# Attention and feed-forward gradients in one kernel: twelve weight-gradient stores go to another queue, three staging buffers in place of four

## The chip, the cores and the metric

The kernel runs on one core of a Trainium2 chip. The metric is device time in microseconds, the median over runs of one launch; a profile shows one execution in detail.

## The reference, cut

The forward pass is `x + A(xn) + B(xn)` with `xn = layernorm(x)`, `x` of 4 x 1 x 512. `A` is one decoding step of attention over the last 1024 of 4096 cached keys and values; `B` is a GELU-gated feed-forward layer of width 1792. Asked for are the output and its gradient by all weights and by both caches.

```python
W = min(4096, max(256, Sk // 4))                 # 1024 of 4096
q = (x @ wq).reshape(B, Sq, Hq, Dh)              # 4 batches, 32 heads of 128
k = jnp.repeat(k_cache[:, :, Sk - W:, :], rep, axis=1)   # 8 kv heads
v = jnp.repeat(v_cache[:, :, Sk - W:, :], rep, axis=1)
p = _softmax(einsum("bhqd,bhkd->bhqk", q, k) * Dh ** -0.5)
a = einsum("bhqk,bhkd->bhqd", p, v).reshape(B, Sq, Hq * Dh) @ wo
b = (_gelu(xn @ w_gate) * (xn @ w_up)) @ w_down
out, vjp = jax.vjp(lambda ...: x + a + b, A_x, A_k_cache, A_v_cache, A_wq, A_wo, B_w_gate, B_w_up, B_w_down)
return (out, *vjp(grad_out))
```

All data are bfloat16. The cache gradients have the full shape 4 x 8 x 4096 x 128: the last 1024 positions of each of the 32 (batch, head) regions hold values, the first 3072 are zero and must be written as zero.

## The kernel before

**What moves.** 30.68 MB are read and 81.01 MB written. Of the written bytes 50.33 MB are the zeros of out_2 and out_3 (`zeros`, from the constant tile `ztile`, in regions of 786 KB, up to four to a transfer), 16.8 MB the computed parts of these two outputs, the rest the weight gradients out_4 to out_8.

**Stages.** First the loads and the feed-forward part: `xnm` and `dym` (`xn` and `dy`, masked by row, L251 to L256, made on POOL), the hidden layer, `f_rows` (L691), which lays the hidden gradients out as rows (`a_r`, `dhg_r`, `dhu_r`), and pieces for out_8, out_6 and out_7 (`piece_d`, `piece_g`). Then a loop over NT = 4 groups of GP = 2 kv heads. Group t runs `masks`, `scores(t, 0)` (keys: PE transposes, then the scores), `softmax`, `scores(t, 1)` (values, for dP), `softmax_d` (its two hooks make dS and its transpose), `pre(t + 1)` for the next group's queries, `odq`, `fin`, then `load_next(t)`, which issues the loads of group t + 2 on POOL's queue.

**Background pieces.** A deque `bg` holds small pieces of work in order: one matmul, one copy out of PSUM by `evac` (ScalarE or VectorE, whichever has the smaller planned load), and after the last piece of a tile the store. `tick(n)` takes n of them and stands between the foreground steps. `dvdk(t, 0)` and `dvdk(t, 1)` (L529) append the pieces of dV and dK, two tiles each, here called dv0, dv1, dk0, dk1; a tile `stg` is 1 MB, takes eight pieces, and comes from the pool `stage` (L760). `dw(t)` (L551) appends the pieces of out_5 (two tiles `osb_o`) and out_4 (two tiles `osb_q`) of 512 KB each, four pieces to a tile, from the pool `outp` with four buffers (L82). They run during group t + 1, and for the last group at the end.

**Queues.** Zeros are issued by ScalarE (ACT) in its own order, at the places that `ZN` (L391) and the calls of `zeros(n)` give: after the second K step of a head in `scores`. SyncE (SP) issues the stores of stg, of the feed-forward outputs and of the small outputs; GpSimd (POOL) the loads from group 1 on and, up to group 2, the stores of `dw`. Each engine issues in program order and waits at a transfer whose data or tile is not ready. A tile that is written again first waits for the landing of the store that read it.

**Tiles that share memory.** `xnm`, `a_r`, `dhg_r` and `dhu_r` use tags of the attention part (`od_x`, `dST`, `E_f`, `Gt`, `dS_x`), so a later attention tile has to wait for their last reader. After the feed-forward part its pools are closed, and `stage` (four tiles of 8 KB per partition) and `wodd` (weights and caches of odd groups) take their memory.

Of the kernel before, what the change touches and what calls it, by code (L numbers as in the profile page):

```python
# [13 lines left out]
BF16 = mybir.dt.bfloat16  # L14
P = 128
# [3 lines left out]
def kernel(  # L19
# [27 lines left out]
    nc = tc.nc  # L47

    B, Sq, D = A_x.shape
# [3 lines left out]
    rep = Hq // G  # L53
# [3 lines left out]
    ND = D // P  # L57
# [4 lines left out]
    NT = G // GP  # L62
    HG = GP * rep
# [5 lines left out]
    CW = HG * Dh  # L69
# [7 lines left out]
    const = ctx.enter_context(tc.tile_pool(name="const", bufs=1))  # L77
    kvp = ctx.enter_context(tc.tile_pool(name="kvp", bufs=3))
    wres = ctx.enter_context(tc.tile_pool(name="wres", bufs=1))
    attw = ctx.enter_context(tc.tile_pool(name="attw", bufs=2))  # L80
# [10 lines left out]
    def evac(out, in_, n, half=False, eng=None):  # L91

        eng = "dve" if half else eng or ("act" if chain else None)
        ca, cd = (190 + n) / 1.2, (120 + (n / 2 if half else n)) / 0.96
        if eng is None:
            eng = "act" if load["act"] + ca <= load["dve"] + cd else "dve"
        load[eng] += ca if eng == "act" else cd
        if eng == "act":
            last.append(nc.scalar.copy(out=out, in_=in_))  # L99
            return last[-1]  # L100
        return nc.vector.tensor_copy(out=out, in_=in_)  # L101

    def store(eng, out, in_, kind, apart):

        d = eng.dma_start(out=out, in_=in_)
        for k in apart:
            tc.declare_no_dep(d.ins, group=k, reason="stores write disjoint parts of the outputs")
        tc.add_to_no_dep_group(kind, d.ins)
        return d
# [14 lines left out]
    wg_sb = ffn_w.tile([P, ND, F], BF16, name="wg_sb")  # L124
    nc.sync.dma_start(out=wg_sb[:], in_=B_w_gate.rearrange("(p c) f -> p c f", p=P))
    wu_sb = ffn_w.tile([P, ND, F], BF16, name="wu_sb")
# [8 lines left out]
    dy_b = const.tile([P, D], BF16, name="dy_b")  # L135
# [10 lines left out]
    msk_i = const.tile([P, rep], FP32, name="msk_i")  # L146
# [86 lines left out]
    xn_b = const.tile([P, D], BF16, name="xn_b")  # L233
# [13 lines left out]
                                  in_=tps[:].rearrange("p c (b r) -> p c b r", b=B)[:, :, :, 0:8])  # L247

    xnm2 = [attw.tile([P, rep // 2, D], BF16, name="xnm", tag=tag, bufs=1) for tag in ("od_x", "dST")]  # L251
    dym = ffn.tile([P, rep, D], BF16, name="dym")
    for src, dst in ((dy_b, [dym[:, i, :] for i in range(rep)]), (xn_b, [xnm2[i // 2][:, i % 2, :] for i in range(rep)])):
        for i in range(rep):
            nc.gpsimd.tensor_scalar(out=dst[i], in0=src[:], scalar1=msk_i[:, i:i + 1], scalar2=None,
                                    op0=ALU.mult)  # L256


# [64 lines left out]
    def tick(n):  # L323
        for _ in range(min(n, len(bg))):
            bg.popleft()()
# [225 lines left out]
    def dw(t):  # L551

        X = st[t]["X"]
        eng = nc.gpsimd if t + 1 < NT else nc.sync

        def piece_o(g, i, held):
            if i == 0:
                held["osb"] = outp.tile([P, rep, D], BF16, name="osb_o", tag="o")
            mps = ps_w.tile([P, D], FP32, name="dwo_ps", tag="w")
            nc.tensor.matmul(mps[:], lhsT=X[:].rearrange("p h d -> p (h d)")[:, g * rep + i:CW:HG], rhs=dyz[:], start=True, stop=True)  # L560
            evac(held["osb"][:, i, :], mps[:], 512)
            if i == rep - 1:
                store(eng, out=out_5[t * CW:(t + 1) * CW, :].rearrange("(p k) n -> p k n", k=HG)[
                    :, g * rep:(g + 1) * rep, :], in_=held["osb"][:], kind="rest", apart=["zeros", "rest"])

        def piece_q(c2, k, held):
            if k == 0:
                held["osb"] = outp.tile([P, 2, GP, rep * Dh], BF16, name="osb_q", tag="o")
            ci, g = k // GP, k % GP
            c = c2 * 2 + ci  # L570
            mps = ps_w.tile([P, rep * Dh], FP32, name="dwq_ps", tag="w")
            nc.tensor.matmul(mps[:], lhsT=xnz[:, c:D:ND],  # L572
                             rhs=X[:, g * rep:(g + 1) * rep, :].rearrange("p i d -> p (i d)"), start=True, stop=True)
            evac(held["osb"][:, ci, g, :], mps[:], 512)
            if k == 2 * GP - 1:
                store(eng,
                      out=out_4.rearrange("(p c) j -> p c j", c=ND)[:, c2 * 2:(c2 + 1) * 2, t * CW:(t + 1) * CW],
                      in_=held["osb"][:].rearrange("p c g j -> p c (g j)"), kind="rest", apart=["zeros", "rest"])

        for g in range(GP):  # L580
            held = {}
            for i in range(rep):
                bg.append(lambda g=g, i=i, held=held: piece_o(g, i, held))
        for c2 in range(ND // 2):
            held = {}
            for k in range(2 * GP):
                bg.append(lambda c2=c2, k=k, held=held: piece_q(c2, k, held))
# [26 lines left out]
    NF4 = (NF + 3) // 4  # L614
# [9 lines left out]
    def ftb(name):  # L624
        t_ = ffn.tile([P, 4 * NF4, B], BF16, name=name)
        nc.vector.memset(t_[:], 0.0)
        return t_
# [52 lines left out]
    aT_b = ftb("aT_b")  # L680
    nc.vector.tensor_tensor(out=aT_b[:, 0:NF, :], in0=gl[:], in1=hu, op=ALU.mult)
    dhuT_b = ftb("dhuT_b")
# [3 lines left out]
    dhgT_b = ftb("dhgT_b")  # L686
# [1 line left out]

    acc_sum(0, [(lambda c, fc=fc: wd_sb[:, fc, c * P:(c + 1) * P], aT_b[:, fc, :]) for fc in range(NF)])

    def f_rows(srcT, nm, tag):  # L691

        ps = od_ps[:]
        for f4 in range(NF4):
            for b in range(B):
                nc.tensor.matmul(ps[b * RB:b * RB + 4, f4, :], lhsT=srcT[:, 4 * f4:4 * f4 + 4, b], rhs=ident[:],
                                 start=True, stop=True, tile_position=(0, b * RB))
        rows = attw.tile([P, NF4, P], BF16, name=nm, tag=tag, bufs=1)
        evac(rows[:], ps, 512)
        return rows  # L700

    a_r = f_rows(aT_b, "a_r", "E_f")
    def piece_d(f4, i, n, held):
        if i == 0:
            held["osb"] = outp.tile([P, 4, D], BF16, name="osb_d", tag="o")
# [8 lines left out]
    def piece_g(s_r, og, c, i, held):  # L714
        if i == 0:
            held["osb"] = outp.tile([P, NF4, 4, P], BF16, name="osb_g", tag="o")
        n = (NF - i + 3) // 4
        mps = ps_w.tile([P, NF4, P], FP32, name="dwg_ps", tag="w")
        nc.tensor.matmul(mps[:, 0:n, :].rearrange("p f d -> p (f d)"), lhsT=xnm2[i // 2][:, i % 2, c:D:ND],  # L719
                         rhs=s_r[:, 0:n, :].rearrange("p f d -> p (f d)"), start=True, stop=True)  # L720
        evac(held["osb"][:, 0:n, i, :], mps[:, 0:n, :], n * P)
        if i == 3:
            store(nc.sync, out=og.rearrange("(p c) f -> p c f", c=ND)[:, c, :],
                                in_=held["osb"][:].rearrange("p f i d -> p (f i d)")[:, 0:F], kind="rest",
                      apart=["zeros", "rest"])

    for f4 in range(NF4):
        held = {}
        n = min(4, NF - 4 * f4)
# [2 lines left out]
    df_ps = ps_a.tile([P, ND, B], FP32, name="df_ps", tag="S")  # L732
    edge = dict(lhsT=ztile[0:1, 0:P], rhs=ztile[0:1, 0:ND * B])
    nc.tensor.matmul(df_ps[:].rearrange("p c b -> p (c b)"), start=True, stop=False, **edge)
    for srcT, wsb, og, nm, tag in ((dhgT_b, wg_sb, out_6, "dhg_r", "Gt"), (dhuT_b, wu_sb, out_7, "dhu_r", "dS_x")):
        s_r = f_rows(srcT, nm, tag)
        for c in range(ND):
            held = {}
            for i in range(4):
                bg.append(lambda s_r=s_r, og=og, c=c, i=i, held=held: piece_g(s_r, og, c, i, held))  # L740
        for f2 in range(NF // 2):
            wT_ps = ps_w.tile([P, 2, ND, P], BF16, name="wgT_ps", tag="w")
            for i in range(2):
                fc = 2 * f2 + i
                for c in range(ND):
                    nc.tensor.transpose(wT_ps[:, i, c, :], wsb[:, c, fc * P:(fc + 1) * P], ident[:])  # L746
            wgT = tsb.tile([P, 2, ND, P], BF16, name="wgT", tag="wT")
            evac(wgT[:], wT_ps[:], 1024, half=True)
            for i in range(2):
                for c in range(ND):  # L750
                    nc.tensor.matmul(df_ps[:, c, :], lhsT=wgT[:, i, c, :], rhs=srcT[:, 2 * f2 + i, :],
                                     start=False, stop=False)
            tick(1)
            if f2 == NF // 2 - 1:
                zeros(4 if og is out_7 else 2)
# [1 line left out]
    acc_add(1, df_ps[:])  # L757

    ffn_pools.close()
    with tc.tile_pool(name="stage", bufs=4, reuse_waits="tile") as stage, \  # L760
            tc.tile_pool(name="wodd", bufs=1, reuse_waits="tile") as wodd:
        wpool.append(wodd)
        kvpool.append(wodd)
# [93 lines left out]
```

## Time and profile before

| What | Value |
|---|---|
| Runs | 281.13, 281.97 and 281.65 us; median 281.65 us |
| Profiled execution | 281.13 us, its span 279.4 us |
| Mean granted TensorE clock | 0.905 |
| Busy share of the span | PE 75%, DVE 57%, ACT 41%, POOL 23% |
| DMA | 112.15 MB in 18655 packets, mean 401 GB/s |
| zero stores of 3 MB | 14, median 22.0 us from issue to landing |
| stg_dv and stg_dk stores of 1 MB | 8 each, median 13.0 and 11.5 us |
| osb_o and osb_q stores of 512 KB on POOL's queue | 6 each, median 36.3 and 35.7 us |
| osb_o and osb_q stores on SP's queue (last group) | 2 each, median 14.0 and 14.1 us |

The span runs from the first to the last instruction. A transfer is divided over the core's sixteen DMA rings; the profile gives the mean busy share of the sixteen. PE is TensorE, DVE VectorE, ACT ScalarE; SPq and ACTq are rows of transfers that these engines issue. In a waiting row the engine named last is the one whose work came last.

### The profile page before, as it was taken

To read this page: it belongs to the slowest core of one execution; us is meant where nothing else is said; L and a number is where in the kernel's file an instruction comes from. 1 tells how busy PE (TensorE), PEld (TensorE's weight loads), DVE (VectorE), ACT (ScalarE), POOL (GpSimd) and SP (SyncE) were. 2 spreads that over 40 slices of the span, in tenths; PEclk is the share of its full clock that TensorE was granted. 3 is DMA by queue.
4 is the path that set the end of the run, shared out by engine and by line. 5 is a ranking of instruction groups with operands and counts; after the bars stand their busy time and mean duration, and the time that the engine had idled before them with its cause. 6 is when DMAs were issued, how large, how long until landed. Compare 5 with 4: busy or idle time off the path is not lost.

```text
span 279.4 us, 7192 instructions
## 1 busy us (share of the span) xinstructions
PE 210.2 (75%) x3126; PEld 136.6 (49%) x3132; DVE 158.4 (57%) x336; ACT 115.1 (41%) x214; POOL 63.7 (23%) x68
## 2 busy tenths in 40 slices
PE   1968976968769799968797978689848777789700
PEld 0856854635435565544465744346634444355300
DVE  6955744726557557645675546477632452667830
ACT  1321643435436246536333535472404433725600
POOL 3890003410200544230007612200520022020000
PEclk9985999979998998999689999999995997999865
DMA  7999999999999999999999999999999999999970
GB/s 237 447 388 430 425 406 402 414 421 427 420 419 427 425 419 419 418 429 432 421 421 364 394 392 429 428 423 421 425 423 427 408 424 424 420 427 424 421 316 20
DMA packets 18655, 112.15 MB, mean 401 GB/s; under 512 B 1456, under 2 KB 5056, under 8 KB 9664
## 3 DMA queue, kind: packets, MB, share of 16 engines
q10 hardware_dynamic: 4400, 50.34, 42.7%
q1 hardware_dynamic: 9808, 38.28, 33.6%
q0 software_dynamic: 4416, 23.07, 20.6%
q8 instruction: 24, 0.39, 0.5%
q14 instruction: 7, 0.06, 0.0%
HBM read 30.68 MB, written 81.01 MB: 400 GB/s over the span
## 4 chain that ended last, share of the span: by engine, by line
PE 45%; DMA 27%; DVE 17%; issue 3%; ACT 2%; POOL 1%; another core or an unknown queue 0%; ACTq 0%; DVEq 0%; SPq 0%
DMA out_dram<-osb_o 18%; PE T_ps L402 9%; PE kv_ps L540 8%; DMA out_dram<-osb_d 6%; PE S_ps L407 5%; DVE T_sb L101 5%; DMA out_dram<-ztile 4%; PE dwo_ps L560 3%; PE acc_ps L213 2%; PE od_ps L512 2%; PE wqT_ps L599 2%; PE woT_ps L339 2%; PE wgT_ps L746 2%; POOL P_x L420 1%; PE dwg_ps L719 1%
## 5 line engine op out<-in xcount | busy, mean ns | idle before, releaser
L101 DVE COPY T_sb<-T_ps 128x1024 bf16<-128x1024 bf16 x64 | 43.9, 690 | 50.0 <-PE T_ps L402 49.5
L99 ACT CAST stg_dv<-kv_ps 128x512 bf16<-128x512 f32 x57 | 30.4, 591 | 27.8 <-PE kv_ps L540 27.8
L99 ACT CAST stg_dk<-kv_ps 128x512 bf16<-128x512 f32 x40 | 22.1, 588 | 37.4 <-PE kv_ps L540 23.9
L540 PE MATMUL kv_ps<-domr,P_x 128*128 128x512 bf16 x63 | 22.7, 431 | 5.4 <-POOL P_x L420 4.9
L387 POOL TENSOR_TENSOR domr<-r,msk 128x512 bf16<-128x512 bf16 x8 | 8.1, 1038 | 70.5 <-DVE r L380 70.5
L402 PEld LDWEIGHTS <-kb 128*128 128x128 bf16 x256 | 18.3, 105 | 10.6 <-issue 7.9
L402 PE MATMUL T_ps<-ident,kb 128*128 128x128 bf16 x256 | 23.4, 232 | 0.0
L99 ACT CAST osb_o<-dwo_ps 128x512 bf16<-128x512 f32 x25 | 14.5, 585 | 19.8 <-PE dwo_ps L560 12.6
L99 ACT CAST osb_g<-dwg_ps 128x512 bf16<-128x512 f32 (+1 forms) x28 | 14.1, 539 | 18.5 <-PE dwg_ps L719 11.4
L402 PE MATMUL T_ps<-ident,vb 128*128 128x128 bf16 x256 | 21.1, 224 | 0.1
L540 PE MATMUL kv_ps<-qmr,dS_x 128*128 128x512 bf16 x60 | 19.7, 412 | 1.8 <-DVE dS_x L420 1.4
L402 PEld LDWEIGHTS <-vb 128*128 128x128 bf16 x256 | 16.2, 101 | 6.6 <-issue 4.3
L407 PE MATMUL S_ps<-T_sb,dom 128*32 128x256 bf16 x128 | 12.7, 386 | 8.3 <-DVE T_sb L101 7.8
L99 ACT CAST osb_q<-dwq_ps 128x512 bf16<-128x512 f32 x25 | 14.0, 589 | 9.8 <-PE dwq_ps L572 5.1
L560 PE MATMUL dwo_ps<-dyz,od_x 128*128 128x512 bf16 x32 | 14.1, 481 | 4.9 <-ACT osb_o L99 4.9
L101 DVE CAST stg_dk<-kv_ps 128x512 bf16<-128x512 f32 x24 | 16.0, 684 | 1.8 <-PE kv_ps L540 1.7
L101 DVE COPY woT<-woT_ps 128x1024 bf16<-128x1024 bf16 x16 | 11.0, 689 | 8.8 <-PE woT_ps L339 8.8
L407 PE MATMUL S_ps<-T_sb,qm 128*32 128x256 bf16 x128 | 13.1, 389 | 3.7 <-DVE T_sb L101 3.7
L101 DVE COPY wqT<-wqT_ps 128x1024 bf16<-128x1024 bf16 x16 | 11.0, 687 | 5.3 <-PE wqT_ps L599 5.2
L101 DVE COPY wgT<-wgT_ps 128x1024 bf16<-128x1024 bf16 x14 | 9.7, 692 | 7.2 <-PE wgT_ps L746 7.2
L407 PEld LDWEIGHTS <-dom 128*32 128x32 bf16 x128 | 5.3, 93 | 17.2 <-issue 15.3
L339 PE MATMUL woT_ps<-ident,wo_sb 128*128 128x128 bf16 x128 | 11.4, 237 | 2.7 <-DVE stg_dv L101 1.9
(216 smaller groups left out, 399.0 us busy)
## 6 DMA issues: line engine op xcount, KB each, us to landing
out_dram<-ztile ACTq DMA_DIRECT2D x14, 3072.0 KB, 22.0
out_dram<-stg_dv SPq DMA_DIRECT2D x8, 1024.0 KB, 13.0
out_dram<-stg_dk SPq DMA_DIRECT2D x8, 1024.0 KB, 11.5
out_dram<-ztile ACTq DMA_DIRECT2D x4, 1536.0 KB, 12.6
kb<-in_A_k_cache_dram POOLq DMA_DIRECT2D x5, 1024.0 KB, 20.3
vb<-in_A_v_cache_dram POOLq DMA_DIRECT2D x5, 1024.0 KB, 25.0
out_dram<-osb_g SPq DMA_DIRECT2D x8, 448.0 KB, 15.3
kb<-in_A_k_cache_dram SPq DMA_DIRECT2D x3, 1024.0 KB, 18.5
```

The source lines that it names most:

```text
L99: last.append(nc.scalar.copy(out=out, in_=in_))
L101: return nc.vector.tensor_copy(out=out, in_=in_)
L213: nc.tensor.matmul(ps[:, c, :], lhsT=lf(c), rhs=rhs, start=(k == 0), stop=(k == len(terms) - 1))
L339: nc.tensor.transpose(wT_ps[:, i, c, :], wo_sb[:, 2 * h2 + i, c * P:(c + 1) * P], ident[:])
L387: nc.gpsimd.tensor_tensor(out=mr[:, g], in0=st[t]["r4"][:, k, :].unsqueeze(1).broadcast_to([P, NQ, Dh]), in1=msk[:, :, g].unsqueeze(2).bro ...
L402: nc.tensor.transpose(T_ps[:, jj, :], blks[(t, g)][:, q * JQ + jj, :], ident[:])
L407: nc.tensor.matmul(ps[b * RG:(b + 1) * RG, :], lhsT=lf[:, b, s * RG:(s + 1) * RG], rhs=T_sb[:, :, b], start=(g == 0 and q == 0), stop=(g = ...
L512: nc.tensor.matmul(od_ps[r0:r0 + rep * B, 0, :], lhsT=pT[:, j % JQ, (j // JQ) * GP + g:P:NS], rhs=blks[(t, g)][:, j, :], start=(j == 0), s ...
L540: nc.tensor.matmul(mps[:].rearrange("p q d -> p (q d)"), lhsT=src[:, jj, :], rhs=mr[:, g].rearrange("p q d -> p (q d)"), start=True, stop= ...
L560: nc.tensor.matmul(mps[:], lhsT=X[:].rearrange("p h d -> p (h d)")[:, g * rep + i:CW:HG], rhs=dyz[:], start=True, stop=True)
L599: nc.tensor.transpose(wT_ps[:, i, c, :], wq_sb[:, c, h * Dh:(h + 1) * Dh], ident[:])
L746: nc.tensor.transpose(wT_ps[:, i, c, :], wsb[:, c, fc * P:(fc + 1) * P], ident[:])
```

## The change

The four feed-forward tiles `xnm`, `a_r`, `dhg_r` and `dhu_r` get buffers of their own in the pool `const`. The stores of `dw` go to SP's queue for every group, not only for the last one: twelve stores of 512 KB move from POOL's queue. The pool `stage` has three buffers in place of four. The change is described as one of the places of the zero stores; `ZN`, `zeros` and its calls are the same in both kernels.

```diff
-    xnm2 = [attw.tile([P, rep // 2, D], BF16, name="xnm", tag=tag, bufs=1) for tag in ("od_x", "dST")]
+    xnm = const.tile([P, rep, D], BF16, name="xnm")
     dym = ffn.tile([P, rep, D], BF16, name="dym")
-    for src, dst in ((dy_b, [dym[:, i, :] for i in range(rep)]), (xn_b, [xnm2[i // 2][:, i % 2, :] for i in range(rep)])):
+    for src, dst in ((dy_b, dym), (xn_b, xnm)):
         for i in range(rep):
-            nc.gpsimd.tensor_scalar(out=dst[i], in0=src[:], scalar1=msk_i[:, i:i + 1], scalar2=None,
+            nc.gpsimd.tensor_scalar(out=dst[:, i, :], in0=src[:], scalar1=msk_i[:, i:i + 1], scalar2=None,
                                     op0=ALU.mult)
...
     def dw(t):
-        eng = nc.gpsimd if t + 1 < NT else nc.sync
...
-                store(eng, out=out_5[t * CW:(t + 1) * CW, :].rearrange("(p k) n -> p k n", k=HG)[
+                store(nc.sync, out=out_5[t * CW:(t + 1) * CW, :].rearrange("(p k) n -> p k n", k=HG)[
...
-                store(eng,
+                store(nc.sync,
                       out=out_4.rearrange("(p c) j -> p c j", c=ND)[:, c2 * 2:(c2 + 1) * 2, t * CW:(t + 1) * CW],
...
-    def f_rows(srcT, nm, tag):
+    def f_rows(srcT, nm):
...
-        rows = attw.tile([P, NF4, P], BF16, name=nm, tag=tag, bufs=1)
+        rows = const.tile([P, NF4, P], BF16, name=nm)
...
-        nc.tensor.matmul(mps[:, 0:n, :].rearrange("p f d -> p (f d)"), lhsT=xnm2[i // 2][:, i % 2, c:D:ND],
+        nc.tensor.matmul(mps[:, 0:n, :].rearrange("p f d -> p (f d)"), lhsT=xnm[:, i, c:D:ND],
...
-    with tc.tile_pool(name="stage", bufs=4, reuse_waits="tile") as stage, \
+    with tc.tile_pool(name="stage", bufs=3, reuse_waits="tile") as stage, \
```

More of the change, by code (lines that the diff above doesn't have):

```diff
@@ L697, in f_rows @@
                                  start=True, stop=True, tile_position=(0, b * RB))
-        rows = attw.tile([P, NF4, P], BF16, name=nm, tag=tag, bufs=1)
+        rows = const.tile([P, NF4, P], BF16, name=nm)
         evac(rows[:], ps, 512)
         return rows
-    a_r = f_rows(aT_b, "a_r", "E_f")
+    a_r = f_rows(aT_b, "a_r")
     def piece_d(f4, i, n, held):
@@ L734 @@
     nc.tensor.matmul(df_ps[:].rearrange("p c b -> p (c b)"), start=True, stop=False, **edge)
-    for srcT, wsb, og, nm, tag in ((dhgT_b, wg_sb, out_6, "dhg_r", "Gt"), (dhuT_b, wu_sb, out_7, "dhu_r", "dS_x")):
-        s_r = f_rows(srcT, nm, tag)
+    for srcT, wsb, og, nm in ((dhgT_b, wg_sb, out_6, "dhg_r"), (dhuT_b, wu_sb, out_7, "dhu_r")):
+        s_r = f_rows(srcT, nm)
         for c in range(ND):
```

## The prediction

> **What bounds the kernel now.** I read the map of the span first, then the queues, then the end of the span in small windows, then the waits, and last the issue times around one group. The map and the queue table:
>
> ```profile
> DMA  7999999999999999999999999999999999999970
> ...
> q10 hardware_dynamic: 4400, 50.34, 42.7%
> q1 hardware_dynamic: 9808, 38.28, 33.6%
> q0 software_dynamic: 4416, 23.07, 20.6%
> ```
>
> The sixteen DMA rings are busy in every slice but the first and the last two, while PE is at 75%, DVE at 57% and ACT at 41%. q10 is ACT's queue (zeros), q1 is SP's, q0 is POOL's. The shares sum to 97.4% with instruction fetch: 112.15 MB at full rate, and that is the span. The chain of waits gives PE 45%, but most of its PE steps run beside a full DMA. How the span ends (stretch, length, busy time of five engines, clock, DMA share, GB/s):
>
> ```profile
> 264.00:268.00 4.00, 0.20 (x2) 0.00 (x0) 3.87 (x9) 0.00 (x0) 0.00 (x0) 0.92 0.99 407
> 268.00:272.00 4.00, 0.00 (x0) 0.00 (x0) 0.00 (x0) 0.00 (x0) 0.00 (x0) 0.50 0.71 280
> 272.00:276.00 4.00, 0.00 (x0) 0.00 (x0) 0.00 (x0) 0.00 (x0) 0.00 (x0) 0.50 0.07 29
> 276.00:280.00 4.00, 0.00 (x0) 0.00 (x0) 0.00 (x0) 0.00 (x0) 0.00 (x0) 0.50 0.03 11
> ```
>
> A share of 0.07 is one ring of sixteen. By the packet records most rings are done at 270.3, one runs on to 278.0: it lags by 7.7 us. So the time is the work of the lagging ring plus any moment in which it has nothing queued. The engines matter only where they leave the rings dry. Their own stalls of today are hidden:
>
> ```profile
> ACT osb_o L99 <- DMA out_dram<-osb_o: 6.5, 2, 5.2
> ...
> ACT osb_q L99 <- DMA out_dram<-osb_q: 4.2, 2, 3.2
> ```
>
> These 10.7 us all fall in group 3 (204.7 to 226.9): its osb tiles wait for stores of group 1, which stand on POOL's queue behind up to 6 MB of loads. The map shows 9 there; they cost nothing.
>
> **The change, part by part.** One fact carries the sum. Following one ring's packets back through the trace, the queues that hold work take strict turns, one packet each: from 201 us on it reads 8 KB (SP), 12 KB (ACT), 4 KB (POOL), again and again. Packets last 0.460 us (12 KB), 0.309 (8 KB), 0.159 (4 KB), 0.084 (2 KB), each starting 3 to 4 ns before its forerunner ends. A 1 MB store is 8 packets of 8 KB per ring, a 3 MB zero store 16 of 12 KB, osb_o 8 of 4 KB. osb_q is 8 of 4 KB on POOL's queue but 16 of 2 KB on SP's (the two of group 3 go there now). So a queue's progress is counted in turns, and small packets are the slow lane.
>
> (1) *xnm, a_r, dhg_r, dhu_r in buffers of their own.* The same four POOL multiplies per source and the same copies. It removes four waits for shared tags; neither the table of waits nor the group rows show one. 0 us, no cover needed; 0 at both ends.
>
> (2) *Twelve stores from POOL to SP.* POOL loses 6 x 0.568 + 6 x 0.727 = 7.8 us of issuing; its next work, P_x at L420, waits for ACT's P_b today (0.6 to 0.9 us), not for POOL, so nothing is gained. SP gains 6 x 0.44 + 6 x 0.68 = 6.7 us of issuing, in gaps where it waits for data. Six osb_q become 96 packets of 2 KB per ring in place of 48 of 4 KB: 96 x 0.0805 - 48 x 0.1555 = **0.3 us** on each ring, and nothing hides it. The 10.7 us of osb waits go: worth 0 by themselves. SP and ACT transfers take eight completion semaphores in turn; the eighth one back is down in every case I counted, closest at the last stores (issue 262.84, the zero store before it down at 261.7): 0, at most 1 us.
>
> (3) *Three staging buffers, with (2).* A group stages dv0, dv1, dk0, dk1. With four buffers dk1 reuses a tile of the group before; with three it takes the tile of its own group's dv0, whose store must be down.
>
> ```profile
> out_dram<-ztile ACTq DMA_DIRECT2D x14, 3072.0 KB, 22.0
> out_dram<-stg_dv SPq DMA_DIRECT2D x8, 1024.0 KB, 13.0
> ...
> out_dram<-osb_q POOLq DMA_DIRECT2D x6, 512.0 KB, 35.7
> ```
> ```profile
> 160.82 0.60 POOL L105 DMA_DIRECT2D out_dram<-osb_o  x1 [0.64 <-ACT osb_o L99]
> 166.36 0.54 POOL L105 DMA_DIRECT2D out_dram<-osb_o  x1 [4.93 <-ACT osb_o L99]
> 169.50 0.72 POOL L105 DMA_DIRECT2D out_dram<-osb_q  x1 [2.60 <-issue]
> 173.35 0.73 POOL L105 DMA_DIRECT2D out_dram<-osb_q  x1 [3.13 <-ACT osb_q L99]
> ```
> ```profile
> 182.81 6.17 SPq L105 DMA_DIRECT2D out_dram<-stg_dv  x2
> 198.71 6.89 SPq L105 DMA_DIRECT2D out_dram<-stg_dk  x2
> ```
> ```profile
> 198.51 1.07 ACT L99 CAST stg_dk<-kv_ps 128x512 bf16<-128x512 f32 x2 [0.36 <-PE kv_ps L540]
> ```
>
> Last column of the first fence: us from issue to landing. The others are issue times in group 2 and the first write of its dk1 (198.5). With dv's 13.0 us alone, dk1 would find the tile free (182.8 + 13 = 195.8). But now dv0 stands on SP behind the four osb stores. SP's turns from 157.4, when dk1 of group 1 is issued: dk1 8, osb_o 8 + 8, osb_q 16 + 16, dv0 8. ACT's zeros issued in that time (158.8, 165.7, 172.2, 180.6): 8 + 16 + 16 + 16 = 56, as many as stand before dv0. So dv0 lands among the last. Work of one ring up to there: SP 16 x 0.306 + 16 x 0.156 + 32 x 0.081 = 10.0; zeros 56 x 0.457 = 25.6; loads 32 x 0.306 + 16 x 0.156 = 12.3; in all 47.9 us, so to 205 on an ordinary ring and some 4 us later on the lagging one: dk1 stalls from 198.5 to about 210. Behind ACT's blocked copy stand the zero stores, which ACT issues itself, and PE once its four PSUM buffers are full.
>
> What is dry, and for how long: when dv0 lands, the rings still hold dv1 and dk0, 16 x 0.306 = 4.9 us. The next store is dk1 itself, 6.55 us after its first write (198.51 to 205.06); the next zero store comes later (211.14 less the 5.2 us wait that is gone: 7.4). With 0.4 us from last packet to landing and 1.4 from issue to first packet (the 4 KB dx_b store takes 1.6 in all): 0.4 + 6.55 + 1.4 - 4.9 = **3.45 us** without data, on every ring, lag or not. If PE works ahead through four PSUM buffers (some 1.5 us) it is 2.0; if dv1 and dk0 are through before, the whole 8.35. I take 3.45: PE works in order and has dk1's matmuls next.
>
> In groups 0 and 1 the same count leaves stalls of 0 to 3 us, covered by zeros and loads still queued. In group 3 osb_q is again ahead of dv0: from the second osb_o's issue 8 x 0.616 + 32 x 0.544 + 8 x 0.766 = 28 us, against some 22 to dk1's first write: 6 us of stall. Four zero stores (29 us) cover it. The last store then leaves at 264.0 - 10.7 + 11 + 6.5 = 270.8, inside the lagging ring's 278 + 3.75; without that cover each further us of stall beyond some 8 counts in full.
>
> **Sum.** 0.3 + 3.45 = 3.75 us on the profiled run's 281.13 (span 279.4): 284.9. The median of the three runs is 0.5 above it, so for a median I say 281.65 + 3.75 = **285.4 us**. The zero stores themselves stay as they are: the diff leaves ZN and every call of zeros() alone, and their times shift with the stalls only.
>
> The row that carries this is one packet per turn: osb_q's 16 packets of a ring alternate one by one. The Trainium skill, "DMA: Bandwidth & Descriptors", section "Queues, rings and completion order", has a ring drain a whole packet of about 9 to 17 descriptors before it switches; osb_q would then pass in one or two turns, dv0 would land in time, and the sum would be 0.3 us. The same page's "Rules for kernel authors" says that spreading transfers over SP, ACT and GpSimd brings no bandwidth since all share the same engines; by it alone a moved store costs nothing. The trace agrees on the sharing, not on the size of a turn.
>
> **Rivals.** *No change* (dv0 in time after all, as osb_q shares turns when loads are through early; for: dv lands in 11.9 to 14.3 us in all eight cases; against: none of these had osb_q ahead of it): 281.65 + 0.3 = 281.95, which is within 0.3%, about the least that a measurement of this kernel can tell from no change.
> *Faster:* the lagging ring lags because of POOL's transfers, whose last ring is late most (osb_q 35.7 us, longest 53.4). If the 7.7 us go by their number, from 28 to 16, the tail loses 7.7 x 12/28 = 3.3: 281.65 + 0.3 - 3.3 = 278.65. For: SP's own transfers spread less (dv within 2.4 us). Against: one slow ring stays behind on SP's last stores too. It decides if the one-ring tail after 270 shrinks below 4 us and no dry stretch appears.
> *Slower still:* dv1 and dk0 are through before dk1 can be written, or the stall of group 3 outlasts the zeros: up to 0.3 + 8.35, 290.3.
>
> **Chances.** Forecast 0.62 (own range 283.5 to 287.0, from the 2.0 and the loss of some more cover), slower still 0.15, no change 0.09, faster 0.14. Hence faster 0.14, same 0.09, slower 0.77. From 281.3 to 290.0 the range takes in the forecast, nearly all of the longer stall and part of no change, and leaves out the faster case: about 0.8.
>
> **What would show it.** Right: a wait of stg_dk for a stg_dv store (some 11 us in group 2, 6 in group 3); no waits of osb for osb; dv landing in 20 to 27 us in groups 2 and 3; one or two slices near 210 to 220 with a DMA digit below 9. Wrong: digits of 9 all through, or stg_dk waiting for nothing. If the dry stretch is there and the time is not longer, the lag of the last ring has shrunk.

## The result, and the profile after

The changed kernel takes **286.23 us** (median of 4 runs, 285.5 to 286.37) against 281.65 us (281.13 to 281.97): the ratio is 1.016, 95% interval [1.0136, 1.0182]. It is slower by 4.6 us. The forecast was 285.4 us. The profiled execution took 286.29 us with a span of 284.5 us, at a granted clock of 0.887.

The map of the span and the queue table of the changed kernel (busy tenths of the DMA rings and GB/s in 40 slices of 7.1 us; per queue packets, MB and share of the rings' time):

```profile
DMA  7999999999999999999999999999990999999994
GB/s 241 441 401 425 423 398 399 418 415 418 427 431 422 423 414 373 422 422 434 418 418 395 350 366 419 434 418 427 419 389 29 416 433 409 435 413 423 427 412 173
DMA packets 19423, 112.15 MB, mean 394 GB/s; under 512 B 1456, under 2 KB 5056, under 8 KB 10432
...
q10 hardware_dynamic: 4400, 50.34, 42.0%
q1 hardware_dynamic: 12304, 44.58, 38.7%
q0 software_dynamic: 2688, 16.78, 15.1%
```

There is one hole: slice 31 has digit 0 and 29 GB/s. The same 112.15 MB move in 768 packets more, those of the six osb_q stores that now go as 2 KB packets. The hole in windows, and the end of the span (stretch, length, busy time of PE, weight load, DVE, ACT and POOL, clock, DMA share, GB/s):

```profile
208.00:212.00 4.00, 0.00 (x0) 0.00 (x0) 0.00 (x0) 0.38 (x1) 0.00 (x0) 0.50 1.01 423
212.00:216.00 4.00, 3.45 (x31) 2.27 (x31) 1.58 (x3) 2.36 (x5) 0.00 (x0) 0.50 0.29 123
216.00:220.00 4.00, 4.00 (x75) 3.17 (x73) 1.72 (x4) 0.84 (x2) 1.42 (x2) 0.50 0.00 0
220.00:224.00 4.00, 4.00 (x43) 2.07 (x40) 2.24 (x5) 2.58 (x5) 0.61 (x1) 0.98 0.97 400
...
276.00:280.00 4.00, 0.00 (x0) 0.00 (x0) 3.39 (x9) 0.00 (x0) 0.00 (x0) 0.77 0.99 393
280.00:284.00 4.00, 0.00 (x0) 0.00 (x0) 0.00 (x0) 0.00 (x0) 0.00 (x0) 0.50 0.15 56
```

Up to 212 the engines stand still and the rings are full; from 213 to 220 the engines work and most rings are empty. Most rings are busy until 279.8 now, where before most were done at 270.3. What the engines waited for (total us, times, longest), all lines of a stg_dk tile for a store:

```profile
ACT stg_dk L99 <- DMA out_dram<-stg_dv: 17.9, 3, 9.4
...
DVE stg_dk L101 <- DMA out_dram<-stg_dv: 3.4, 1, 3.4
```

This wait did not exist before, and the waits of osb for osb are gone. Where the longest falls, by ACT's and SP's timelines (start, length, what; idle before it, and its releaser):

```profile
201.62 0.58 ACT L99 CAST stg_dk<-kv_ps 128x512 bf16<-128x512 f32 x1 [3.74 <-PE wqT_ps L597]
211.62 1.07 ACT L99 CAST stg_dk<-kv_ps 128x512 bf16<-128x512 f32 x2 [9.42 <-DMA out_dram<-stg_dv]
...
220.91 0.63 ACTq L105 DMA_DIRECT2D out_dram<-ztile  x1
```
```profile
186.85 6.17 SPq L105 DMA_DIRECT2D out_dram<-stg_dv  x2
202.77 17.00 SPq L105 DMA_DIRECT2D out_dram<-stg_dk  x2
```

dv0 of group 2 is issued at 186.85 and lands at 211.53, 24.7 us later; the copy into dk1 starts 0.09 us after that. The second stg_dk of the last line, dk1, is issued at 219.24. Between dk0 (202.77) and dk1 nothing at all is handed to the rings, because the next zero store (220.91) stands on ACT behind the blocked copies.

### The profile page after: what moved, and what is told of

Its sections match the earlier page's. It is cut to its first block, busy times and chain, and to the rows that moved or that the text cites. A ratio compares the mean times of both kernels' runs of the same rounds, so it can differ in the third digit from the quotient of the medians.

```text
span 284.5 us, 7183 instructions
## 1 busy us (share of the span) xinstructions
PE 212.9 (75%) x3126; PEld 139.1 (49%) x3132; DVE 159.5 (56%) x336; ACT 114.9 (40%) x214; POOL 56.0 (20%) x56
## 2 busy tenths in 40 slices
DMA packets 19423, 112.15 MB, mean 394 GB/s; under 512 B 1456, under 2 KB 5056, under 8 KB 10432
## 4 chain that ended last, share of the span: by engine, by line
PE 46%; DMA 27%; DVE 15%; ACT 4%; issue 3%; POOL 2%; ACTq 0%; DVEq 0%; SPq 0%
DMA out_dram<-stg_dv 22%; PE T_ps L401 9%; PE kv_ps L539 6%; PE S_ps L406 5%; DVE T_sb L101 5%; DMA out_dram<-osb_g 5%; PE dwo_ps L558 3%; PE acc_ps L213 3%; PE wgT_ps L744 3%; POOL P_x L419 2%; PE woT_ps L338 2%; ACT stg_dk L99 2%; PE dwg_ps L717 2%; PE dwq_ps L570 1%; PE wqT_ps L597 1%
## 5 line engine op out<-in xcount | busy, mean ns | idle before, releaser
L539 PE MATMUL kv_ps<-qmr,dS_x 128*128 128x512 bf16 x60 | 21.4, 432 | 17.4 <-ACT stg_dk L99 15.2
L401 PE MATMUL T_ps<-ident,kb 128*128 128x128 bf16 x256 | 23.5, 233 | 0.0
L401 PE MATMUL T_ps<-ident,vb 128*128 128x128 bf16 x256 | 21.3, 226 | 0.1
L419 POOL TENSOR_TENSOR P_x<-P_b,bmsk 128x1024 bf16<-128x1024 bf16 x4 | 7.6, 1892 | 58.5 <-ACT P_b L467 58.5
L539 PEld LDWEIGHTS <-dS_x 128*128 128x128 bf16 x64 | 5.4, 101 | 17.2 <-issue 14.4
L597 PEld LDWEIGHTS <-wq_sb 128*128 128x128 bf16 x128 | 8.7, 101 | 10.1 <-issue 8.4
## 6 DMA issues: line engine op xcount, KB each, us to landing
out_dram<-stg_dv SPq DMA_DIRECT2D x8, 1024.0 KB, 19.1
out_dram<-ztile ACTq DMA_DIRECT2D x4, 1536.0 KB, 13.4
out_dram<-osb_q SPq DMA_DIRECT2D x8, 512.0 KB, 23.2
```

The costliest lines, as they stand in the source:

```text
L401: nc.tensor.transpose(T_ps[:, jj, :], blks[(t, g)][:, q * JQ + jj, :], ident[:])
L419: eng.tensor_tensor(out=dst[:].rearrange("p j (m b) -> p (j m) b", b=B), in0=src[:].unsqueeze(2).broadcast_to([P, WQ, B]), in1=bmsk[:].uns ...
L539: nc.tensor.matmul(mps[:].rearrange("p q d -> p (q d)"), lhsT=src[:, jj, :], rhs=mr[:, g].rearrange("p q d -> p (q d)"), start=True, stop= ...
L597: nc.tensor.transpose(wT_ps[:, i, c, :], wq_sb[:, c, h * Dh:(h + 1) * Dh], ident[:])
```

## The experiments

Each is given as its difference from one of the two kernels. Ratios are to the kernel before, run beside it on the same chip (medians there 281.42 to 281.47 us).

**Each half of the change alone.** Before, with three staging buffers:

```diff
-    with tc.tile_pool(name="stage", bufs=4, reuse_waits="tile") as stage, \
+    with tc.tile_pool(name="stage", bufs=3, reuse_waits="tile") as stage, \
```

> The kernel before with three staging buffers as its only edit; the twelve stores stay on POOL's queue. Theory (the wait comes from dv0 standing behind osb_q on SP's queue, so three buffers alone do little): dv0's store in groups 2 and 3 lands some 13 us after issue, at 196 and 252, when dk1's first writes are due at 198.5 and 252; waits of stg_dk for stg_dv stay under 1.5 us in total, the osb waits of 10.7 us stay, time 281.2 to 282.3. Rival (one buffer less is the whole cost): waits of 15 us or more, 285 to 287.

Measured: 281.06 us (280.58 to 282.99), ratio 0.9996 [0.9976, 1.0015]. dv lands in 12.0 to 14.1 us, no tile of stg waits for a store, and no slice of the map is below 9 between the first and the tail. The osb waits sum to 6.4 us, not the 10.7 expected. Three buffers alone cost nothing.

Before, with the twelve stores on SP's queue and four buffers:

```diff
-        eng = nc.gpsimd if t + 1 < NT else nc.sync
+        eng = nc.sync
```

> The kernel before with the twelve stores on SP's queue as its only edit; four staging buffers and the shared tags stay. Theory: dk1 takes a buffer of the group before, so no stg_dk waits for a store although dv0 lands 19 to 25 us after issue; the osb waits are gone; the rings stay busy throughout; the 2 KB packets cost 0.3 us: 281.3 to 282.6. Rival (small packets on SP's queue are the cost): 285 to 286.5. Rival (POOL's transfers make the last ring lag): below 280.

Measured: 281.84 us (281.0 to 282.61), ratio 1.001 [0.9996, 1.0025]. Issues of this kernel, then the end of its span:

```profile
out_dram<-stg_dv SPq DMA_DIRECT2D x8, 1024.0 KB, 25.0
...
out_dram<-osb_q SPq DMA_DIRECT2D x8, 512.0 KB, 28.2
```
```profile
268.00:272.00 4.00, 0.00 (x0) 0.00 (x0) 0.00 (x0) 0.00 (x0) 0.00 (x0) 0.50 0.72 283
272.00:276.00 4.00, 0.00 (x0) 0.00 (x0) 0.00 (x0) 0.00 (x0) 0.00 (x0) 0.50 0.09 35
276.00:280.00 4.00, 0.00 (x0) 0.00 (x0) 0.00 (x0) 0.00 (x0) 0.00 (x0) 0.50 0.03 12
```

dv's median landing nearly doubles, from 13.0 to 25.0 us (32.1 at the longest, later than expected), and with a fourth buffer no stg_dk waits for a store. The osb waits are not all gone, as was expected: 3.5 us of osb_q are left, and one copy into a stg_dv tile waits 3.4 us for a store. The time shows neither. The tail is that of before (0.71, 0.07, 0.03): the last ring still ends at 278.0, though twelve of 28 transfers left POOL's queue. The rival "faster", which needed a shorter tail, falls. So each half is free; only together do they cost.

**Own tiles and three buffers, all twelve stores on POOL's queue** (the changed kernel with the old choice of queue):

```diff
-                store(nc.sync, out=out_5[...
+                store(nc.gpsimd if t + 1 < NT else nc.sync, out=out_5[...
...
-                store(nc.sync,
+                store(nc.gpsimd if t + 1 < NT else nc.sync,
```

> The changed kernel with all twelve stores back on POOL's queue: tiles of their own for xnm, a_r, dhg_r and dhu_r, and three staging buffers, are what is left of the change. Theory (these tiles cost and bring nothing): as the kernel before with three buffers, 280.6 to 282.3, a DMA map of 9 throughout. Rival (the tiles take part in the loss): above 283.

Measured: 281.4 us (280.27 to 282.08), ratio 0.9995 [0.9975, 1.0014]. The four tiles of their own cost nothing.

**Which of the moved stores does it.** The changed kernel with only osb_q back on POOL's queue (the second of the two edits above):

> The changed kernel with only the six osb_q stores back on POOL's queue; the osb_o stores stay on SP, three staging buffers. Theory (turns count, and osb_q has 32 of the 56 turns ahead of dv0): dv0 of group 2 lands some 15 us after issue, stg_dk waits 3 us or less in total, no slice of the map below 9, time 281.5 to 283. Rival (any store moved to SP costs its share of bytes): half of the loss remains, 283.5 to 284.5.

Measured: 282.0 us (280.61 to 282.85), ratio 1.0012 [0.999, 1.0033]. dv lands in 11.2 to 17.4 us; stg_dk waits for no store; the map shows 9 all through up to the tail. With only osb_o back (the first of the two edits):

> The changed kernel with only the six osb_o stores back on POOL's queue; the osb_q stores, in 2 KB packets, stay on SP. Theory (turns): 40 turns in place of 56 stand before dv0 of group 2, it lands some 17 to 21 us after issue, stg_dk waits 2 to 6 us in group 2, and the dry stretch is short or gone: 281.8 to 284. It lies between the kernel with osb_q on POOL (282.0) and the changed one (286.2). Rival (the packets' size alone is the cost): 285.5 to 286.5.

Measured: 283.56 us (282.12 to 284.5), ratio 1.0068 [1.0044, 1.0092]. The time is in what was expected, the rest is not: dv0 of group 2 lands after 23.5 us, later than said, ACT's stg_dk waits sum to 15.2 us (longest 8.3), and the hole stays (one slice with digit 2 and 86 GB/s). So osb_q's 32 packets of 2 KB per ring are what makes dv late, and osb_o's 16 of 4 KB add little: dv0 lands 1.2 us earlier without them. By the packet records all sixteen rings are empty together for 2.2 us there (216.8 to 219.0), against 4.4 us in the changed kernel.

**The turn by packets.** The changed kernel with zero packets of 6 KB in place of 12 KB, so twice as many and each shorter; all bytes as before:

```diff
-    ZP = P // 2
+    ZP = P
```

> The changed kernel with the zero stores read from 128 partitions in place of 64, so in packets of 6 KB, twice as many. Theory (queues take turns of one packet): SP's 56 turns before dv0 of group 2 now pass 56 packets of 6 KB, some 13 us less than with 12 KB; dv0 lands 15 to 19 us after issue in place of 24.7, stg_dk waits 4 us or less in group 2, and zeros are left to fill the rings, so the dry stretch is gone. 256 more packets per ring cost some 2.8 us: 284 to 286. Rival (a turn is a batch of bytes or of several packets): dv0 lands as before, the wait of 9 us and the dry stretch stay, 288 to 290.

Measured: 288.43 us (287.22 to 290.24), ratio 1.0262 [1.0214, 1.031]: a miss in time. Its map and two issue lines:

```profile
DMA  7999999999999999999997899999999999999990
...
out_dram<-stg_dv SPq DMA_DIRECT2D x8, 1024.0 KB, 10.3
...
out_dram<-osb_q SPq DMA_DIRECT2D x8, 512.0 KB, 14.4
```

The turn shows as predicted: if every packet of ACT's queue is half as long, SP's queue advances faster. dv's median landing is 10.3 us instead of 19.1, osb_q's 14.4 instead of 23.2, stg_dk waits for no stg_dv store, and the hole in slice 31 is gone. The time is lost elsewhere: there are 23519 packets, and those of the zeros take 121.1 us of a ring in place of 119.4; another hole opens in slices 22 and 23 (digits 7 and 8), where a mean ring idles 3.2 us between 150 and 160 us, against 0.5 in the changed kernel; and slices 15 to 17 move only 375, 368 and 347 GB/s. Why is open.

**Filling the hole while the wait stays.** The changed kernel, with a zero store of 3 MB taken from group 3's first K step and put behind softmax_d of group 2, ahead of the blocked copies:

```diff
-    ZN = ((0, 4, 4, 4), (0, 4, 4, 2), (2, 4, 4, 4), (4, 4, 4, 4))
+    ZN = ((0, 4, 4, 4), (0, 4, 4, 2), (2, 4, 4, 4), (0, 4, 4, 4))
...
-            zeros(4 if t == NT - 1 else 0)
+            zeros(4 if t >= NT - 2 else 0)
```

> The changed kernel with one zero store of four regions issued earlier: at the end of group 2's softmax_d in place of the first K step of group 3. Theory (the loss is the dry stretch of about 6.6 us on an average ring and 3.5 us on the last one, not the stall): stg_dk still waits 8 us or more for the store of stg_dv in group 2, but 16 more packets of 12 KB (7.3 us) keep the rings busy: 281.8 to 283.5. Rival (the stalls lengthen the chain of the engines, and that is what sets the end): 285.5 to 287.

Measured: 283.2 us (281.5 to 284.03), ratio 1.0065 [1.0045, 1.0085]. stg_dk still waits 13.4 us in all, 10.9 at the longest, and some 3 of the 4.6 us are back. The hole is shallower, not gone: two slices with digit 6, the second where the store taken away is missing, right behind the stall. So the zeros were then taken from elsewhere, once from group 0's last step (first line below), once from the two half stores around the turn from group 1 to group 2 (second line); the call of zeros stays as above:

```diff
-    ZN = ((0, 4, 4, 4), (0, 4, 4, 2), (2, 4, 4, 4), (4, 4, 4, 4))
+    ZN = ((0, 4, 4, 0), (0, 4, 4, 2), (2, 4, 4, 4), (4, 4, 4, 4))
+    ZN = ((0, 4, 4, 4), (0, 4, 4, 0), (0, 4, 4, 4), (4, 4, 4, 4))
```

> The changed kernel, but one zero store of 3 MB (four regions) is taken from the last K step of group 0's value scores and put behind softmax_d of group 2, just ahead of the blocked dk1 copies; group 3 keeps all of its zero stores. Theory (the three or so us of the change are rings that run dry while ACT stands before dk1): the wait of stg_dk for stg_dv stays (8 to 12 us in group 2), but the rings now hold 16 more packets of 12 KB each, 7.3 us of work, in that stretch. Both slices near 212 to 220 show a DMA digit of 8 or 9, and unlike the run with a zero taken from group 3 there is nothing missing behind the stall: 281.5 to 283.0 us. Rival (the wait itself costs the time, since it delays every later step): 285 to 287 with the wait there, whatever the DMA digit. Rival (early zeros were needed where they were): a digit below 9 near 60 to 80 us, and 284 or more.

Measured: 282.85 us (281.94 to 284.6), ratio 1.0062 [1.0039, 1.0085]. From ACT's timeline and the map:

```profile
209.57 1.07 ACT L99 CAST stg_dk<-kv_ps 128x512 bf16<-128x512 f32 x2 [12.39 <-DMA out_dram<-stg_dv]
```
```profile
DMA  7999999999999999999989999999997999999994
GB/s 233 445 396 425 425 404 373 405 403 414 426 425 417 389 376 329 432 425 423 423 357 310 392 423 423 429 429 420 419 426 326 422 414 430 416 421 430 417 415 174
```

The wait in group 2 is 3 us longer than in the changed kernel, and the time 3.4 us shorter. Between 210 and 220 a ring idles 1.6 us on average instead of 6.65. Slice 31 still has a 7, where 8 or 9 was expected. And this execution, 1.4 us slower than the kernel's median, loses time early: slices 14 to 16 fall to 389, 376 and 329 GB/s (changed kernel: 423, 414, 373), and slice 21 has a digit of 8. The theory holds for the hole; that the zeros were missed where they had been, the third rival, is likely but not shown.

> As the run before, but the four regions come from two stores of two regions each: group 1's last value step and group 2's first key step (near 120 to 150 us), closer to the stall. Theory: 24 packets of 8 KB or 12 KB less stand ahead of group 2's dv0 in time, the wait of stg_dk for stg_dv may be some us shorter, the digits near 212 to 220 are 8 or 9, 281.5 to 283.0 us. Rival (the wait itself costs): 284.5 to 287 while a wait of more than 6 us is there.

Measured: 282.04 us (281.1 to 283.18), ratio 1.0012 [0.9994, 1.0031]: the change without its cost. Its waits and its map:

```profile
ACT stg_dk L99 <- DMA out_dram<-stg_dv: 16.2, 3, 7.8
...
DVE stg_dk L101 <- DMA out_dram<-stg_dv: 6.5, 1, 6.5
```
```profile
DMA  6999999999999999999999999999999999999891
```

ACT and DVE wait 22.7 us for stg_dv stores, more than in the changed kernel (21.3), though ACT's wait in group 2 is 5.8 us in place of 9.4. The rings idle 0.7 us between 210 and 220 and 1.0 near 265, and the time is that of before. A wait of the engines costs nothing here; empty rings do.

**The lagging ring.** To see whether the late ring can be relieved, the kernel before with its last zero region written through four rings only:

```diff
+    def zeros_few(n, k):
+        zs = ztile[0:P:P // k, :]
...
+            kk = ZP // k
+            zsrc = bass.AP(tensor=zs.tensor, offset=zs.offset, ap=[list(zs.ap[0]), [0, kk], [1, ZW]])
...
-            zeros(4 if t == NT - 1 else 0)
+            zeros(3 if t == NT - 1 else 0)
+            if t == NT - 1:
+                zeros_few(1, 4)
```

> The kernel before, with the last of the 64 zero regions (786 KB) written through four rings in place of sixteen: source rows from four partitions, outermost size four. It asks whether the one ring that runs on after 270 us sets the end. If so, and if it is none of these four: the other twelve lose 4 packets of 12 KB each (1.8 us), the four gain 12 (5.5 us) and end near 276, so the kernel ends some 1.5 us earlier: 279.5 to 280.5. Rival (the last transfers or the small stores behind them set the end, not one ring's work): 281 to 283. If the late ring is one of the four: 286 to 288.

Measured: 292.06 us (291.55 to 293.44), ratio 1.0374 [1.0346, 1.0403], worse than any case expected. The end of its span:

```profile
276.00:280.00 4.00, 0.00 (x0) 0.00 (x0) 0.00 (x0) 0.00 (x0) 0.00 (x0) 0.50 0.26 94
280.00:284.00 4.00, 0.00 (x0) 0.00 (x0) 0.00 (x0) 0.00 (x0) 0.00 (x0) 0.50 0.18 59
284.00:288.00 4.00, 0.00 (x0) 0.00 (x0) 0.00 (x0) 0.00 (x0) 0.00 (x0) 0.50 0.14 54
```

Four rings of sixteen (0.25) run on to 287 to 288.5 while the others end at 273 to 277. It shows that the last ring's work sets the end, here with four last rings; it does not show which ring lagged, nor a gain. No kernel tried beats the one before.

## Why the prediction was right

**The bound.** The prediction took the time as the work of the last ring plus its empty moments. Ring ends from the packet records, in the profiled executions (some of these lie at the low or the high end of their kernel's runs):

| Kernel | Idle of a mean ring, 200 to 270 us | Most rings end | Last ring ends | This execution |
|---|---|---|---|---|
| before | 0 | 270.3 | 278.0 | 281.13 |
| zeros from the turn of groups 1 and 2 | 1.7 | 273.0 | 277.7 | 281.10 |
| zeros from group 3 | 4.6 | 276.2 | 278.1 | 281.50 |
| zeros from group 0 | 1.6 | 277.7 | 280.9 | 284.26 |
| osb_o back on POOL | 5.6 | 278.5 | 281.2 | 284.45 |
| changed | 7.1 | 279.8 | 282.9 | 286.29 |

In each the time is the last ring's end plus 3.1 to 3.4 us. A mean idle of up to 4.6 us in this stretch left the last ring's end where it was; 5.6 us moved it by 3.2, and 7.1 us by 4.9. The row with zeros from group 0 does not fit this order: its last ring ends 2.9 us late with little idle after 200. It lost the time earlier: from 84 to 113 us its rings moved 380 GB/s, where the kernel with zeros from the turn of groups 1 and 2 moved 421.

**The sum.** 0.3 us for the small packets: both kernels that carry osb_q's 2 KB packets without a hole (four buffers: 1.001 [0.9996, 1.0025]; refilled hole: 1.0012 [0.9994, 1.0031]) agree with it, and with nothing as well. Own tiles at 0 and the osb waits at 0 hold. The hole is 4.4 us on the last ring where 3.45 was said: its last packet ends at 216.07, and all rings start again between 220.43 and 220.58. The miss is one term. Filling dk1 was put at 6.55 us, as before, and took 7.6 (211.62 to 219.24), most likely because PE came back at half its clock. PE's groups of dk1's matmuls in the kernel before and in the changed one (minimum, median, maximum in ns):

```profile
L540 PE MATMUL kv_ps<-qmr,dS_x x9: 376/377/379, 197.4 to 203.9; 128*128 128x512 bf16 x9
```
```profile
L539 PE MATMUL kv_ps<-qmr,dS_x x6: 582/631/634, 212.3 to 217.8; 128*128 128x512 bf16 x6
```

With that, 0.3 + 4.4 = 4.7 of the 4.9 us by which the last ring ends later; the other 0.2 is not assigned.

**The step that was wrong:** "without data, on every ring, lag or not". On a middle ring the hole is 7.4 us (213.1 to 220.5). A buffer comes free when the *last* ring has written its share of dv0 (211.53); by then the others have long done theirs and part of dv1 and dk0 too, so a middle ring holds some 1.5 us more, not the 4.9 us that the sum subtracts. The last ring catches up meanwhile: its lag falls from 7.7 to 3.1 us. The total came out because that ring sets the end, and for it the sum was right but for the fill of dk1.

**The signs.** The wait in group 2 is 9.4 us (11 said), in group 3 4.7 (6), in group 1 3.8 (0 to 3), the last two covered as said. dv0 lands in 24.7 us in group 2 (20 to 27 said), but in 16.7 in group 3, so that group was costed too dear. One packet per turn shows in the changed kernel itself: between 187 and 203 us a mean ring moves 29.1 packets of 2 KB from SP's queue and 28.4 of 12 KB from ACT's. Two kernels confirm it, one with other turns and one with shorter ones: osb_q off the queue gives landings of dv in 11 to 17 us, shorter zero packets 9 to 14. The Trainium skill, "DMA: Bandwidth & Descriptors", section "Queues, rings and completion order", has a ring drain some 9 to 17 descriptors of one queue before it switches; by that osb_q's packets would have passed in a turn or two and dv would have landed in time, and these runs disagree. Its "Rules for kernel authors", that spreading transfers over queues brings no bandwidth, agrees with the run of the move alone (1.001).

**The rivals.** "No change" would have been right with either half alone. (The prediction has dv land in 11.9 to 14.3 us "in all eight cases" before; the trace gives the landing of three of the eight stores, and these are in that range.) "Faster" fell with the unchanged tail. "Slower still" needed the whole 8.35 us on the last ring; dv1 and dk0 covered it as the forecast said.

## What to carry to other kernels

Where the transfers are the bound, a long wait of an engine is harmless as long as the queues hold more work than the wait lasts; ask what has been issued by the moment it begins, and whether the engine that blocks is also the one that issues the filler. A queue's delay goes by the number of packets ahead of it and by how long the other queues' packets are, not by its own bytes, so small packets put ahead of a store that holds a scarce buffer are the thing to look for. Two edits that are each free can cost together: a buffer less is free while stores land early, and late stores are free while there is a buffer more.

## What the runs showed of the hardware that was not expected

- After 8.5 us without work PE's granted clock was 0.50 and stayed there up to 220 us, about 8 us beyond its return, and a 128x512 matmul took 631 ns in place of 377.
- A ring that lags by 7.7 us at the end catches up while the others are empty: a hole of 4.6 us on a mean ring left the last ring's end at 278.1.
- 786 KB through four rings instead of sixteen cost 10.6 us; 12 KB packets there lasted up to 1.81 us, against 0.89 at the longest in the kernel before.
- Halving the packets of the zeros sped up SP's queue (dv's median landing 19.1 to 10.3 us), but their time on a ring grew from 119.4 to 121.1 us, and the kernel was slower still.
